# Cached grouped-query attention on one core: where the last V block stands among the wo loads

## The chip, the core and the metric

The kernel runs on one core of a Trainium2 chip. A core has five engines with instruction queues of their own: TensorE (PE, matrix products), VectorE (DVE), ScalarE (ACT), GpSimd (POOL) and SyncE (SP). Here SP issues nearly every load from HBM. The metric is the device time of one execution in microseconds. Before the change its median over 6 runs is 189.66 us (189.29 to 191.03).

## The reference

```python
B, Sq, D = 8, 4, 512;  Hq, Hkv, Sk, Dh = 32, 8, 2048, 128
q = (x @ wq).reshape(B, Sq, Hq, Dh).transpose(0, 2, 1, 3)
k = jnp.repeat(k_cache, 4, axis=1)          # (B, 32, 2048, 128)
v = jnp.repeat(v_cache, 4, axis=1)
p = softmax(einsum("bhqd,bhkd->bhqk", q, k) * Dh ** -0.5)
o = einsum("bhqk,bhkd->bhqd", p, v)
out = o.transpose(0, 2, 1, 3).reshape(B, Sq, Hq * Dh) @ wo      # (8, 4, 512)
```

All inputs are bf16. The two caches are 33.6 MB each and wq and wo are 4.2 MB each, so some 75.5 MB have to be read.

## The kernel before, in words

The work is cut into 32 units of one batch entry and one pair of kv heads; unit u has pair p = u // 8 and batch b = u % 8. Each unit needs one K block and one V block of 1 MB. A software pipeline (the loop at L488) runs step n with three units in hand: PE transposes the K block of unit n (L215; DVE and ACT copy the result out of PSUM, L216), unit n-1 gets its scores and their exponential (L286, L296) and its probabilities are turned to keys (L306), and unit w = n-2 gets the product with V (`values`, L343, for the last twenty units) and is scaled into oT (`finish`, L354). `norms` (L328, L336) makes the reciprocal sums for two units at a time.

The output projection with wo is folded into this loop by quarters of 1024 rows of wo, one for each pair p. `to_tokens` (L428 transposes, L434 copy) and `to_wo_rows` (L450 transposes, L452 copy) bring oT into the row order in which wo is loaded; each needs the one before it. `project(p, r0, n)` (L480) then issues two matmuls for each of n row groups, all of them accumulating into the one PSUM tile out_ps. The last ones are followed by one copy on ACT (L542) and two stores of 16 KB (L543, L544).

Quarter 0 of wo is laid out in three pieces: wo_e (eight small loads early in the kernel), and what is called its last small rows here: wo_n (64 rows, 64 KB, L141) and wo_m (640 rows, 640 KB, L142), both loaded by `load_wo_m`. Quarters 1 to 3 lie in wo_sb. `load_wo(p, r0, n)` (L148) loads n of the eight row groups of quarter p. Quarter 1 and quarter 2 come in two loads of 512 KB each (called 1a, 1b, 2a, 2b here), quarter 3 in four of 256 KB (3a to 3d).

All of these loads stand in SP's one queue in the order in which the program issues them. A list `loads`, built ahead of the loop (L153 to L163), fixes that order for K, V, and some of the wo loads; `load_ready` (L165) issues from it at each step as far as buffers allow (seven K, six V). SP also waits before each load until the load eight places before it has landed: there are eight completion semaphores for loads, used in turn. So about eight loads are always outstanding. The end of SP's order before the change is

```
... V28, K31, V29, V30, V31, wo_n, wo_m, 1a, 1b, 2a, 2b, 3a, 3b, 3c, 3d, output store
```

The order of work on each engine is written by hand: the pool is set to a manual schedule (L71), and an engine runs its instructions in program order. At the end of the loop, step w = 30 issues `values(30)`, `norms(30)`, `finish(30)` and then, on L531 to L533, `project(0, 8, 6)` (rows of wo_m and wo_n, 12 matmuls) and `project(1, 0, 8)` (16 matmuls). Only then comes step w = 31 with `values(31)`, the consumer of V31. After the loop come `to_tokens(2)`, `to_wo_rows(2)`, and the projections of quarters 2 and 3 (32 matmuls).

Of the kernel before, what the change touches and what calls it, by code (L numbers as in the profile page):

```python
# [14 lines left out]
def kernel(  # L15
# [27 lines left out]
    NU = G2 * B  # L43
# [3 lines left out]
    KA = A + 1  # L47
# [85 lines left out]
    def load_wo_e(i):  # L133

        hi, m = divmod(i, 4)
        rows = wo[: NE * WE, :].rearrange("(q r) j -> q r j", r=WE)
        a, b = hi * 32 + m, hi * NE // 2 + m
        nc.sync.dma_start(wo_e[a : a + 17 : 4, :, :], rows[b : b + 17 : 4, :, :])

    def load_wo_m():  # L140
        nc.sync.dma_start(wo_n[:, :], wo[HP * 128 - WN : HP * 128, :])  # L141
        nc.sync.dma_start(  # L142
            wo_m[:, :, :], wo[NE * WE : HP * 128 - WN, :].rearrange("(q r) j -> q r j", r=WM)
        )

    def load_wo(p, r0, n):
        rows = wo[p * HP * 128 : (p + 1) * HP * 128, :].rearrange("(q r) j -> q r j", r=WR)
        nc.sync.dma_start(wo_sb[:, p - 1, r0 : r0 + n, :], rows[:, r0 : r0 + n, :])  # L148
# [4 lines left out]
    loads = []  # L153
    for u in range(NU + KA):
        if 1 <= u <= 8:
            loads.append(("e", u - 1))
        if 0 < u < NU:
            loads.append(("k", u))
        if u == NU + 2:
            loads += [("m", 0), ("w", 0), ("w", 4)]  # L160
        if u >= KA - 1 and u - KA + 1 < NU:
            loads.append(("v", u - KA + 1))
    loads.reverse()  # L163

    def load_ready(nk, nv):  # L165

        while loads:
            kind, u = loads[-1]
            if kind in "emw":
                loads.pop()  # L170
                load_wo_e(u) if kind == "e" else load_wo_m() if kind == "m" else load_wo(1, u, 4)
                continue
            if u >= (nk + KB if kind == "k" else nv + VB):
                return
            loads.pop()
            (load_k if kind == "k" else load_v)(u)
# [30 lines left out]
    def transpose_part(u, part):  # L207
        t, half = divmod(part, 2)
        if half == 0:
            kt[(u, t)] = ktpool.tile([128, JT, 128, 2], BF16, tag="kt", name="kt")  # L210
        kp = psum_k.tile([128, JT // 2, 128], FP32, tag="k", name="kp")
        k4 = ks[u][:, :, :].rearrange("s c d -> s (c d)").bitcast(FP32)
        for j in range(JT // 2):
            w = (part * JT // 2 + j) * 128
            nc.tensor.transpose(kp[:, j, :], k4[:, w : w + 128], ident4[:, :])  # L215
        (nc.scalar.copy if part == 3 else nc.vector.tensor_copy)(  # L216
            out=kt[(u, t)][:, half * JT // 2 : (half + 1) * JT // 2, :, :].rearrange(
                "k j s e -> k (j s e)"
            ),
            in_=kp[:, :, :].rearrange("k j s -> k (j s)").bitcast(BF16),  # L220
        )
# [93 lines left out]
    def sums_by_query(u):  # L315
        by_gq = small.tile([128, 2, 2, HQ], FP32, tag="by_gq", name="by_gq")
        nc.vector.tensor_tensor(
            out=by_gq[:, :, :, :],
            in0=l_sbs[u][:, :].unsqueeze(2).unsqueeze(2).to_broadcast([128, 2, 2, HQ]),
            in1=by_q[:, :, :].unsqueeze(1).to_broadcast([128, 2, 2, HQ]),  # L320
            op=mybir.AluOpType.mult,
        )
        by_qs[u] = by_gq
# [100 lines left out]
    def to_tokens(n):  # L424
        rows = len(groups[n]) * T
        nat = psum_l.tile([rows, HP, 128], BF16, tag="l", name="nat")
        for h in range(HP):
            nc.tensor.transpose(  # L428
                nat[:, h, :], oT[n][:, h, :, :, :].rearrange("d p b s -> d (p b s)"), ident[:, :]
            )  # L430
        flat = nat[:, :, :].rearrange("t h d -> t (h d)")
        nats[n] = nat_sb[:rows, : HP * 128 + (n == 0) * 24 * WE]
        if n > 0:
            nc.vector.tensor_copy(out=nats[n][:, :], in_=flat)  # L434
            return

        w = 32 * WE
        nc.vector.tensor_copy(out=nats[0][:, :w], in_=flat[:, :w])
        nc.vector.tensor_copy(
            out=nats[0][:, w : 2 * w], in_=flat[:, NE // 2 * WE : NE // 2 * WE + w]  # L440
        )
        nc.vector.tensor_copy(out=nats[0][:, 2 * w :], in_=flat[:, NE * WE :])

    def to_wo_rows(n):
        rows = len(groups[n]) * T
        if n > 0:
            perm = psum_l.tile([128, WR, rows], BF16, tag="l", name="perm")
            by_row = nats[n][:, :].rearrange("t (q r) -> t r q", r=WR)
            for r in range(WR):
                nc.tensor.transpose(perm[:, r, :], by_row[:, r, :], ident[:rows, :rows])  # L450
            to = oP3[:, :, :] if n == 2 else oP12[:, :, :, :].rearrange("q r p t -> q r (p t)")
            nc.vector.tensor_copy(out=to, in_=perm[:, :, :])  # L452
            return

        perm = psum_l.tile([128, WE + WM + 1, T], BF16, tag="l", name="perm")
        w = 64 * WE
        by_row = nats[0][:, :w].rearrange("t (q r) -> t r q", r=WE)
        for r in range(WE):
            nc.tensor.transpose(perm[:64, r, :], by_row[:, r, :], ident[:T, :T])
        by_row = nats[0][:, w : w + 128 * WM].rearrange("t (q r) -> t r q", r=WM)  # L460
        for r in range(WM):
            nc.tensor.transpose(perm[:, WE + r, :], by_row[:, r, :], ident[:T, :T])
        nc.tensor.transpose(perm[:WN, WE + WM, :], nats[0][:, w + 128 * WM :], ident[:T, :T])
        nc.vector.tensor_copy(out=oN[:, :], in_=perm[:WN, WE + WM, :])
        nc.vector.tensor_copy(out=oE[:, :, :], in_=perm[:64, :WE, :])
        nc.vector.tensor_copy(out=oM[:, :, :], in_=perm[:, WE : WE + WM, :])

    def project(p, r0, n):

        for r in range(r0, r0 + n):  # L470
            if p > 0:
                o, w = oP[p][:, r], wo_sb[:, p - 1, r]
            elif r < WE:
                o, w = oE[:, r, :], wo_e[:, r]
            elif r < WE + WM:
                o, w = oM[:, r - WE, :], wo_m[:, r - WE]
            else:
                o, w = oN[:, :], wo_n
            for half in range(2):
                nc.tensor.matmul(  # L480
                    out_ps[half * T : (half + 1) * T, :],
                    lhsT=o,
                    rhs=w[:, half * DH : (half + 1) * DH],
                    start=(p == 0 and r == 0),
                    stop=(p == G2 - 1 and r == WR - 1),
                )

    for n in range(NU + A):  # L488
        w = n - A
        for part in range(2):  # L490
            if 0 < n < NU:
                transpose_part(n, part)
        if 2 <= w <= NU - NS and w % 2 == 0:
            finish2(w - 2)
        if 0 < w < NU - NS and w % 2:
            sums_by_row(w - 1)
        if 0 <= n - 1 < NU:
            scores(n - 1)
        for part in range(2, 4):
            if 0 < n < NU:  # L500
                transpose_part(n, part)
        if w >= NU - NS and w % 2 == 0:
            sums_by_query(w)
        if 0 <= n - 1 < NU:
            probs_to_keys(n - 1)
        if w >= 0:
            p, b = units[w]
            if p in (1, 3) and b == 1:
                to_tokens(p // 2)
            if w >= NU - NS:  # L510
                values(w)
                if w % 2 == 0:
                    norms(w)
                finish(w)
            elif w % 2 == 1:
                values2(w - 1)
            if p in (1, 3) and b == 2:
                to_wo_rows(p // 2)
        load_ready(min(n + 1, NU), max(w + 1 if w >= NU - NS else (w + 1) // 2 * 2, 0))
        if w == NU - 1 - VB:  # L520
            assert not loads
            load_wo(2, 0, 4)
            load_wo(2, 4, 4)
            for r in range(0, WR, 2):
                load_wo(3, r, 2)

        if w == 13:
            out_ps = psum_e.tile([2 * T, DH], FP32, tag="e", name="out_ps")
        if 14 <= w < 18:
            project(0, (w - 14) * 2, 2)  # L530
        if w == NU - 2:  # L531
            project(0, WE, WM + 1)
            project(1, 0, 8)  # L533

    to_tokens(2)
    to_wo_rows(2)
    project(2, 0, 4)
    project(2, 4, 4)
    for r in range(0, WR, 2):
# [35 lines left out]
```

## Time and profile before

| what | value |
|---|---|
| median of 6 runs | 189.66 us |
| the profiled execution itself | 196.64 us |
| its span, first to last instruction | 194.9 us |
| PE, DVE, ACT busy | 143.7, 132.4, 62.4 us |
| bytes moved by DMA, mean rate over the span | 75.86 MB, 389 GB/s |
| rate from 0 to 80 us, from 80 to 177 us | 384 GB/s, 425 GB/s |
| rate from 177 to 184.5 us | 377 GB/s |
| granted TensorE clock, mean | 0.959 |

Times in the views are microseconds from the start of the span. "PE kp L215" is an instruction of PE that writes tile kp, recorded for line 215. In a timeline a row has its start, its length, engine, line, operation, output and inputs, the number of instructions that were merged, and in brackets how long the engine had been idle before and what ended that. A load's row on SP is its issue; it lands later. The profiled execution is 7.0 us longer than the median, so differences are worked out in it and then taken from the median.

### The profile page before, as it was taken

The numbers are of one execution on the slowest core, as the hardware profiler recorded it, in microseconds if no ns is written. First come the engines' busy times: TensorE is split into PE (matmuls) and PEld (weight loads), VectorE is DVE, ScalarE is ACT, GpSimd is POOL, SyncE is SP. The second block draws the span as 40 slices with busy tenths as digits, with TensorE's granted clock in tenths as the row PEclk, the third lists the DMA queues.
The fourth block names the chain that finished last, engine by engine and source line by source line (L and its number), as shares of the span: only waits on it lengthen the run. The fifth ranks groups of instructions, "written<-read, shape, count | busy, mean of one in ns | idle before, by whom it ended". The sixth has DMA issues, their size and how long they took to land.

```text
span 194.9 us, 4854 instructions
## 1 busy us (share of the span) xinstructions
PE 143.7 (74%) x2090; PEld 114.7 (59%) x2090; DVE 132.4 (68%) x260; ACT 62.4 (32%) x110; POOL 4.6 (2%) x9
## 2 busy tenths in 40 slices
PE   0706699798885979998787887777777787874673
PEld 0602167677674767887666666666666576763362
DVE  0840459978866579787978785878787887886020
ACT  2011245443523343434333333333333332432000
POOL 8000000000000000000000000000000000000000
PEclk9999999999999699999999999999999999998585
DMA  6999999999999999999999999999999999999940
GB/s 254 432 403 391 392 382 394 382 394 385 392 383 394 382 394 380 415 425 424 422 424 429 425 425 425 425 419 427 422 429 424 429 422 429 424 428 379 380 182 7
DMA packets 10980, 75.86 MB, mean 389 GB/s; under 512 B 1288, under 2 KB 1448, under 8 KB 2600
## 3 DMA queue, kind: packets, MB, share of 16 engines
q1 hardware_dynamic: 10912, 75.55, 95.8%
q8 instruction: 16, 0.26, 0.5%
q14 instruction: 4, 0.03, 0.0%
q10 hardware_dynamic: 48, 0.02, 0.0%
HBM read 75.53 MB, written 0.03 MB: 388 GB/s over the span
## 4 chain that ended last, share of the span: by engine, by line
DMA 92%; PE 4%; SPq 1%; DVE 0%; issue 0%; ACT 0%
DMA k_sb<-in_k_cache_dram 51%; DMA v_sb<-in_v_cache_dram 26%; DMA wo_sb<-in_wo_dram 8%; DMA wq_sb<-in_wq_dram 7%; PE out_ps L480 2%; PE kp L215 1%; SPq L118 1%; PE o_ps L343 0%; DVE nat_sb L434 0%; PE perm L450 0%; PE nat L428 0%; PE s_ps L286 0%; ACT out_sb L542 0%; SPq L128 0%; DVE oT L354 0%
## 5 line engine op out<-in xcount | busy, mean ns | idle before, releaser
L215 PE MATMUL kp<-ident,k_sb 128*128 128x128 f32 x512 | 72.2, 288 | 29.7 <-DMA k_sb<-in_k_cache_dram 28.7
L215 PEld LDWEIGHTS kp<-ident,k_sb 128*128 128x128 f32 x512 | 58.4, 147 | 40.9 <-issue 19.0
L216 DVE COPY kt<-kp 128x1024 bf16<-128x1024 bf16 x96 | 63.2, 687 | 26.1 <-PE kp L215 25.8
L306 DVE STREAM_TRANSPOSE probs<-s_sb 64x512 bf16<-64x512 bf16 x64 | 44.9, 702 | 0.6
L296 ACT ACTIVATE s_sb<-s_ps 128x512 bf16<-128x512 f32 x32 | 19.1, 598 | 72.5 <-PE s_ps L286 72.5
L216 ACT COPY kt<-kp 128x1024 bf16<-128x1024 bf16 x32 | 32.4, 1013 | 16.8 <-PE kp L215 16.8
L286 PE MATMUL s_ps<-kt,q_bd 128*32 128x256 bf16 x512 | 21.1, 282 | 0.0
L343 PE MATMUL o_ps<-probs,v_sb 128*128 128x32 bf16 x640 | 19.2, 176 | 1.5 <-DMA v_sb<-in_v_cache_dram 1.5
L343 PEld LDWEIGHTS <-v_sb 128*128 128x128 bf16 x640 | 18.6, 96 | 2.6 <-DMA v_sb<-in_v_cache_dram 2.0
L286 PEld LDWEIGHTS <-q_bd 128*32 128x32 bf16 x512 | 10.7, 95 | 5.6 <-issue 4.5
L381 PE MATMUL o_ps<-v_sb,probs 128*64 128x256 bf16 x192 | 12.0, 279 | 0.0
L381 PEld LDWEIGHTS <-probs 128*64 128x64 bf16 x192 | 10.3, 112 | 1.2 <-issue 1.0
L354 DVE TENSOR_TENSOR oT<-o_ps,r_sb 128x32 bf16<-128x32 f32 x20 | 3.8, 191 | 7.7 <-PE o_ps L343 7.1
L401 ACT ACTIVATE o_sb<-o_ps,r_sb 128x256 f32<-128x256 f32 x6 | 2.8, 474 | 11.7 <-DVE r_sb L399 11.7
L296 ACT ACTIVATION_READ_ACCUMULATOR s_sb<-s_ps 128x1 f32 x32 | 6.2, 194 | 0.0
L336 DVE RECIPROCAL r_sb<-l_ps 128x64 f32<-128x64 f32 x10 | 5.6, 557 | 0.3
L480 PE MATMUL out_ps<-wo_sb,oP 128*32 128x256 bf16 x48 | 5.2, 390 | 0.2 <-DMA wo_sb<-in_wo_dram 0.2
L252 DVE COPY qT_all<-qtp 128x128 bf16<-128x128 bf16 x8 | 1.2, 217 | 5.8 <-PE qtp L246 5.8
L542 ACT CAST out_sb<-out_ps 64x256 bf16<-64x256 f32 x1 | 0.4, 366 | 14.9 <-PE out_ps L480 14.9
L410 PE MATMUL f_ps<-fold,o_sb 128*128 128x64 f32 x24 | 3.7, 279 | 1.6 <-ACT o_sb L401 1.6
L227 PE MATMUL xtp<-ident,x_sb 32*128 32x32 bf16 x4 | 0.3, 194 | 6.2 <-DMA x_sb<-in_x_dram 6.2
L410 PEld LDWEIGHTS f_ps<-fold,o_sb 128*128 128x128 f32 x24 | 3.1, 190 | 2.4 <-ACT o_sb L401 2.1
(59 smaller groups left out, 65.1 us busy)
## 6 DMA issues: line engine op xcount, KB each, us to landing
k_sb<-in_k_cache_dram SPq DMA_DIRECT2D x32, 1024.0 KB, 19.5
v_sb<-in_v_cache_dram SPq DMA_DIRECT2D x32, 1024.0 KB, 14.2
wq_sb<-in_wq_dram SPq DMA_DIRECT2D x1, 4096.0 KB
wo_sb<-in_wo_dram SPq DMA_DIRECT2D x4, 512.0 KB
wo_sb<-in_wo_dram SPq DMA_DIRECT2D x4, 256.0 KB, 8.6
wo_m<-in_wo_dram SPq DMA_DIRECT2D x1, 640.0 KB
wo_e<-in_wo_dram SPq DMA_DIRECT2D x8, 40.0 KB
wo_n<-in_wo_dram SPq DMA_DIRECT2D x1, 64.0 KB, 18.0
```

The source lines that it names most:

```text
L215: nc.tensor.transpose(kp[:, j, :], k4[:, w : w + 128], ident4[:, :])
L216: (nc.scalar.copy if part == 3 else nc.vector.tensor_copy)(out=kt[(u, t)][:, half * JT // 2 : (half + 1) * JT // 2, :, :].rearrange("k j s ...
L286: nc.tensor.matmul(s_ps[y * 32 : (y + 1) * 32, t * JT : (t + 1) * JT, :], lhsT=q_bd[:, p, e, b, y // 2, :, :], rhs=kt[(u, t)][:, :, y * 32 ...
L296: nc.scalar.activation(out=s_sb[:, :, :], in_=s_ps[:, :, :], func=EXP, accum_out=l_sbs[u][:, u % 2 : u % 2 + 1],)
L306: nc.vector.transpose(out=pr[rows, :, g, :], in_=s_sbs[u][rows, :, :].rearrange("q j s -> q (j s)"))
L336: nc.vector.reciprocal(r_sb[:, :, :], l_ps[:, :, :])
L343: nc.tensor.matmul(o_ps[:, :], lhsT=vs[u][:, c, :], rhs=pr[:, c, :, :].rearrange("s g q -> s (g q)"), start=(c == 0), stop=(c == C - 1),)
L354: nc.vector.tensor_tensor(out=oT[(p + 1) // 2][:, :, (p == 2) * 1, b, :], in0=o_pss[u][:, :].rearrange("d (h s) -> d h s", h=HP), in1=r_sb ...
L381: nc.tensor.matmul(o_ps[i * 64 : (i + 1) * 64, :], lhsT=probs[(u + i) % len(probs)][:, c : c + 2, :, :].rearrange("s c g q -> s (c g q)"), ...
L401: nc.scalar.mul(out=o_sb[:, :, :].rearrange("q c d -> q (c d)"), in_=o_ps[:, :], mul=r_sb[:, 0:1])
L410: nc.tensor.matmul(f_ps[:, :, :].rearrange("d u q -> d (u q)"), lhsT=o_sbs[u][:, c, :], rhs=fold[:, c, :, :].rearrange("k u q -> k (u q)") ...
L480: nc.tensor.matmul(out_ps[half * T : (half + 1) * T, :], lhsT=o, rhs=w[:, half * DH : (half + 1) * DH], start=(p == 0 and r == 0), stop=(p ...
```

## The change

The loads of wo_n and wo_m move one place forward in SP's queue, ahead of V31 instead of behind it. Loads 1a and 1b leave the list `loads` and are issued right behind it, with 2a to 3d; their place is still behind V31. On PE, `project(1, 0, 8)` leaves the step w = 30 and is cut in two: its first four row groups come after the transposes of `to_tokens(2)`, its last four after those of `to_wo_rows(2)`. `project(0, 8, 6)` stays ahead of `values(31)`. No instruction is added or taken away: PE, DVE, ACT and SP issue the same ones as before.

```diff
@@ the list of loads
-        if u == NU + 2:
-            loads += [("m", 0), ("w", 0), ("w", 4)]
+        if u == NU + KA - 2:
+            loads.append(("m", 0))
         if u >= KA - 1 and u - KA + 1 < NU:
             loads.append(("v", u - KA + 1))
@@ load_ready
-            if kind in "emw":
+            if kind in "em":
                 loads.pop()
-                load_wo_e(u) if kind == "e" else load_wo_m() if kind == "m" else load_wo(1, u, 4)
+                load_wo_e(u) if kind == "e" else load_wo_m()
                 continue
@@ the loop
         if w == NU - 1 - VB:
             assert not loads
+            load_wo(1, 0, 4)
+            load_wo(1, 4, 4)
             load_wo(2, 0, 4)
             load_wo(2, 4, 4)
@@ its end, and what follows it
         if w == NU - 2:
             project(0, WE, WM + 1)
-            project(1, 0, 8)
 
     to_tokens(2)
+    project(1, 0, 4)
     to_wo_rows(2)
+    project(1, 4, 4)
     project(2, 0, 4)
     project(2, 4, 4)
```

The end of SP's order after the change is

```
... V28, K31, V29, V30, wo_n, wo_m, V31, 1a, 1b, 2a, 2b, 3a, 3b, 3c, 3d, output store
```

and that of PE's is values(30), project(0, 8, 6), values(31), to_tokens(2), 1a's rows, to_wo_rows(2), 1b's rows, 2a to 3d.

## The prediction

> **What bounds the kernel now.** I read the page's slices first, then the chain that ended last in order of time, then the timeline of the last 18 us.
>
> ```profile
> PEclk9999999999999699999999999999999999998585
> DMA  6999999999999999999999999999999999999940
> GB/s 254 432 403 391 392 382 394 382 394 385 392 383 394 382 394 380 415 425 424 422 424 429 425 425 425 425 419 427 422 429 424 429 422 429 424 428 379 380 182 7
> ```
>
> The sixteen DMA engines are full until the last three slices of 4.9 us. Until then only bytes count, and this change moves none. What can be won lies at the end, where the transfers stop and the core is still at work. The rate also says why this execution took 196.64 us and not 189.66: 384 GB/s until 80 us, 425 after it. 80 x (1 - 384/425) is 7.7 us, more than the whole difference of 7.0, so that lies in the head, and the tail can be taken as it stands.
>
> ```profile
> 169.46 14.93 DMA wo_sb<-in_wo_dram
> 184.40 0.04 issue
> 184.44 1.04 PE out_ps L480 x8
> 185.47 0.94 PE o_ps L343 x32
> 186.41 0.02 issue
> 186.44 0.20 DVE oT L354
> ...
> 188.07 0.67 PE perm L450 x8
> 188.74 3.07 PE out_ps L480 x32
> 191.82 0.02 issue
> 191.84 0.37 ACT out_sb L542
> ```
>
> The chain leaves the DMA with load 1b, which lands at 184.40. From there PE and DVE alone set the end, 7.4 us to the copy at 191.84. `values(31)` stands behind the 1b matmuls on PE, so it starts at 185.41.
>
> ```profile
> 177.02 0.96 PE L343 MATMUL o_ps<-probs,v_sb 128*128 128x32 bf16 x32 [0.85 <-DMA v_sb<-in_v_cache_dram]
> 181.71 1.25 PE L480 MATMUL out_ps<-wo_m,oM 128*32 128x256 bf16 x10 [3.46 <-DMA wo_m<-in_wo_dram]
> 183.21 1.04 PE L480 MATMUL out_ps<-wo_sb,oP 128*32 128x256 bf16 x8
> 185.41 0.99 PE L343 MATMUL o_ps<-probs,v_sb 128*128 128x32 bf16 x32
> ```
>
> PE idles 3.46 us for wo_m. V31 is in the core by then: a load waits for the one eight places before it, so SP's issues tell landings. 3a (176.99) waits for V30, 3b (179.83) for V31, 3d (181.69) for wo_m. V31 therefore lay unused for 185.41 - 179.83 = 5.6 us.
>
> ```profile
> 179.83 0.81 SPq L148 DMA_DIRECT2D wo_sb<-in_wo_dram  x2
> 180.20 0.43 SPq L148 DMA_DIRECT2D wo_sb<-in_wo_dram  x1
> 181.69 0.33 SPq L148 DMA_DIRECT2D wo_sb<-in_wo_dram  x1
> ```
>
> The trace's landing records (the last of sixteen increments of a load's semaphore) fill in the rest: V30 176.98, V31 179.81, wo_n 180.13, wo_m 181.67, 1a 183.02, 1b 184.40, 2a 185.67, 2b 186.90, 3a 187.52, 3b 188.14, 3c 188.76, 3d 189.38. The page has one of them as 8.6 us after issue: 180.20 + 8.6 = 188.8, which is 3c. So the last bytes are there 2.4 us before the copy starts. These 2.4 us, less the last four matmuls, are all that an order of work can win.
>
> **The change, part by part.** *Loads.* wo_n took 0.32 us of the stream (179.81 to 180.13) and wo_m 1.54. Placed behind V30 they land at 177.30 and 178.84, and V31 1.86 us later than now, at 181.67. From 1a on every load has the same bytes ahead of it and keeps its time. SP issues as many loads, and each still waits for the eighth before it; five megabytes and more stay outstanding, so the small wo_n taking a place earlier leaves no hole. V31 also waits for its buffer, free once `values(25)` is done; the present issue at 159.69 shows it free two places sooner than it will be asked for. Cost of this part: V31 late by 1.86 us, hidden while nothing needs it before 181.67, otherwise one for one.
>
> *A rule against it.* The Trainium skill, "DMA: Bandwidth & Descriptors" (Anatomy of one DMA), puts some 2.0 us of fixed time on each DMA, fitted there on the GpSimd path, with bytes over 436 GB/s on top, and its rules for authors call transfers under 64 KB mostly overhead. By that, wo_n (64 KB) costs 2.15 us and wo_m 3.5, and V31 lands at 185.5. By the rows here the two cost 1.86 us, since eight loads overlap their fixed parts. I take the rows; the rule's number is the slow rival's.
>
> *PE, step w = 30.* `project(0, 8, 6)` can start at 178.88 instead of 181.71. Its 12 matmuls took 1.50 us (181.71 to 183.21) at the half clock, so they end by 180.4, and PE waits for V31 with nothing behind it that could run.
>
> *PE and DVE, from V31.* `values(31)` takes 0.99 (185.41 row) whatever the clock: that row lies across the rise of the clock at 185.65, and matmuls came as fast before as after. 181.71 to 182.70. oT 0.19 plus gaps as now: transposes of nat at 182.97. These took 0.62 at full clock; at half I allow 1.0 (bounds 0.62 and 1.24): 183.97. The nat_sb copy, 0.68, runs to 184.69. Under it lie the eight matmuls of 1a, landed at 183.02. At half clock eight took 1.04 from first start to last end, 0.42 of it the last one's own length, so a pair starts every 0.21 and eight hold PE 0.85: 183.75 to 184.6. Their cover is the DVE copy; without it they would cost 0.85. Perm transposes 0.67: 184.74 to 185.4. Their copy to oP3 (0.29) lies under 1b's eight matmuls, to 186.2 (1b landed at 184.40).
>
> *The last 32 matmuls.* At the half clock each eight take 0.85, or start with their load. 2a 186.2 to 187.05 (landed 185.67), 2b to 187.9 (186.90), 3a, four in 0.43, to 188.33, 3b to 188.75, 3c from 188.80 (188.76) to 189.2, 3d from 189.42 (189.38). PE has caught up with the loads with about 0.2 us to spare. The last four end 0.21 + 0.42 later: 190.07. The copy starts at 190.1 instead of 191.84: 1.75 us less.
>
> *The clock.* It was granted at half from 179.0 to 185.65, in full to 189.2 and at half again, in steps of 6.65 and 3.55 us. "TensorE: Matmul & The Clock Gate" (Part 1) says that the clock falls after an idle window of some 3.4 us and returns after a busy one, and that the windows run free. By this PE, mostly busy from 181.7 on, has its full clock from about 185.8 to the end, and the last four end 0.4 after 3d: 189.82, 2.0 us less. But the row shows a fall at 189.2 after a window in which PE was busy 2.54 of 3.60 us, so less than a whole idle window sufficed. I take half clock as the safe case; the two differ by 0.25 us, since the loads hold PE in both.
>
> *Sum.* -1.75 (half clock) to -2.0 (full). A tail that runs at the 425 GB/s of the stretch before it, and not at 377, has 3d land 1.1 us sooner after V30 (12.4 x 0.9 = 11.3), while the old chain, 7.4 us fixed after 1b, comes 0.7 sooner: -2.3 then. I take -1.85: **187.8 us**.
>
> **The rivals.**
>
> *Slower: the small loads hold V31 back.* From the start of `values(31)` the old path to the copy takes 6.43 us (185.41 to 191.84), and 1b's matmuls add 0.85. It decides from a start at 191.84 - 7.28 = 184.55, which is a landing 2.85 us later than 181.67; past that it is lost one for one. With the rule's 185.5 the copy is at 192.8: +0.95, **190.6 us**. For it: V30 to V31 took 2.83 us where V29 to V30 took 2.64, so loads near the small ones do run slower. Against: the small loads' own 1.86 us.
>
> *No change that can be measured: PE falls behind the loads.* If transposes and `values` run slower at the half clock than I allow (nat 1.24, perm 1.0, values 1.5), the matmuls get to 2a 1.1 us later. Nothing catches up, the end comes 0.9 later, and the gain is 0.85: **188.8 us**. For it: half clock for 6.65 us, and only 0.2 us of slack. Against: the unchanged pace of `values` across the rise.
>
> *The order does nothing.* If the last loads set the end already, nothing moves: **189.7 us**. Against: 3d is there 2.4 us early, and the chain does not pass through it.
>
> *More: the tail's loads run at 425 GB/s in ordinary executions*, and PE keeps up: -2.3, **187.35 us**. For it: this execution was the slow kind.
>
> **How the numbers follow.** Forecast 0.76, faster tail 0.08, PE behind 0.09, nothing 0.03, slower 0.04. About 0.5%, 0.95 us, is what a measurement of this kernel can tell from no change. PE behind lies on that border and goes to "same" with the third case: faster 0.84, same 0.12, slower 0.04. The range takes in the fast tail with 0.3 for the spread of medians, and PE behind: 187.05 to 188.8.
>
> **What would show it.** V31 lands after wo_m, near 4.7 us after V30. The idle time of PE ahead of the wo_m matmuls is under 1 us instead of 3.46, and a new one of about 1.3 stands ahead of `values(31)`. That starts 3.7 us earlier against V30's landing. The 1a matmuls lie under the nat_sb copy. The chain leaves the DMA at 3d, with four matmuls and the copy behind it, or still shows PE without a gap from V31 on, if the clock stays at half. I am wrong if V31 lands over 2 us later than wo_m plus its own bytes (2.8), if 3d lands later than 12.4 us after V30, or if PE reaches 3d after it has been there for over half a microsecond.

## The result, and the profile after

The changed kernel takes 188.93 us (median of 28 runs), the kernel before 190.95 in the 63 runs that stand beside it; in some executions of either the loads of the first 80 us run slower, so the comparison is made on the undisturbed ones: a ratio of 0.9939, 95% interval 0.9915 to 0.9962. That is 0.6% less, or 1.2 us. The shortest executions are 188.42 and 189.29. The forecast was 187.8 (0.990 of 189.66) with a range up to 188.8, so the sign was right and the gain was put too high.

The profiled execution of the changed kernel takes 191.62 us, with a span of 189.8. The end of its chain of work, in order of time (start, length, what):

```profile
161.97 16.90 DMA v_sb<-in_v_cache_dram
178.87 0.02 issue
178.89 7.44 DMA wo_sb<-in_wo_dram
186.33 0.04 issue
186.37 0.41 PE out_ps L480 x4
186.78 0.02 issue
186.81 0.37 ACT out_sb L545
```

The chain now stays with the loads until 3d, the last one, at 186.33. Behind it lie four matmuls and the copy, nothing else. In the first trace of before it left the loads at 1b, and seven steps of PE and DVE came between that landing and the copy.

The timeline of PE in the changed kernel:

```profile
174.88 1.03 PE L343 MATMUL o_ps<-probs,v_sb 128*128 128x32 bf16 x32 [1.33 <-DMA v_sb<-in_v_cache_dram]
175.75 0.67 PE L328 MATMUL l_ps<-by_gq,ones 128*128 128x64 f32 x2
176.48 1.25 PE L480 MATMUL out_ps<-wo_m,oM 128*32 128x256 bf16 x10
177.66 0.40 PE L480 MATMUL out_ps<-wo_n,oN 64*32 64x256 bf16 x2
178.92 1.03 PE L343 MATMUL o_ps<-probs,v_sb 128*128 128x32 bf16 x32 [0.86 <-DMA v_sb<-in_v_cache_dram]
...
182.66 3.47 PE L480 MATMUL out_ps<-wo_sb,oP 128*32 128x256 bf16 x36
186.37 0.40 PE L480 MATMUL out_ps<-wo_sb,oP 128*32 128x256 bf16 x4 [0.24 <-DMA wo_sb<-in_wo_dram]
```

The wait of 3.46 us for wo_m is gone. `values(31)` starts at 178.92, 4.1 us after V30 has landed (174.84 by the landing records) and not 8.4 us after it as in the first trace of before. PE reaches 3d with 0.24 us in hand.

The windows of the same tail (length, busy time of PE, PEld, DVE, ACT, POOL, then clock, DMA share, GB/s):

```profile
175.00:178.90 3.90, 3.00 (x46) 2.10 (x44) 1.67 (x4) 0.00 (x0) 0.00 (x0) 0.50 1.00 413
178.90:182.66 3.76, 3.46 (x56) 2.85 (x56) 0.87 (x2) 0.00 (x0) 0.00 (x0) 0.50 0.98 387
182.66:186.33 3.67, 3.48 (x38) 2.40 (x37) 0.29 (x1) 0.00 (x0) 0.00 (x0) 0.65 0.45 175
```

PE had half its clock from 174.97 to 185.21, nearly all of this, and the end still came with the loads.

### The profile page after: what moved, and what is told of

It reads as the page before. It is cut to its first block, busy times and chain, and to the rows that moved or that the text cites. A ratio compares the mean times of both kernels' runs of the same rounds, so it can differ in the third digit from the quotient of the medians.

```text
span 189.8 us, 4854 instructions
## 1 busy us (share of the span) xinstructions
PE 143.3 (76%) x2090; PEld 114.8 (60%) x2090; DVE 132.0 (70%) x260; ACT 62.4 (33%) x110; POOL 4.6 (2%) x9
## 4 chain that ended last, share of the span: by engine, by line
DMA 96%; PE 1%; SPq 0%; issue 0%; ACT 0%
DMA k_sb<-in_k_cache_dram 58%; DMA v_sb<-in_v_cache_dram 27%; DMA wq_sb<-in_wq_dram 7%; DMA wo_sb<-in_wo_dram 4%; PE kp L215 1%; SPq L118 0%; PE s_ps L286 0%; PE out_ps L480 0%; ACT out_sb L545 0%; SPq L128 0%
## 5 line engine op out<-in xcount | busy, mean ns | idle before, releaser
L381 PE MATMUL o_ps<-v_sb,probs 128*64 128x256 bf16 x192 | 11.6, 274 | 0.0
L401 ACT ACTIVATE o_sb<-o_ps,r_sb 128x256 f32<-128x256 f32 x6 | 2.8, 474 | 11.3 <-DVE r_sb L399 11.3
L243 ACT ACTIVATE q_nat<-psq 128x512 bf16<-128x512 f32 x2 | 1.2, 597 | 10.3 <-PE psq L236 10.3
```

The source lines that it names most:

```text
L381: nc.tensor.matmul(o_ps[i * 64 : (i + 1) * 64, :], lhsT=probs[(u + i) % len(probs)][:, c : c + 2, :, :].rearrange("s c g q -> s (c g q)"), ...
L401: nc.scalar.mul(out=o_sb[:, :, :].rearrange("q c d -> q (c d)"), in_=o_ps[:, :], mul=r_sb[:, 0:1])
```

## The experiments

Two theories were set against each other. The clock theory: the tail of the kernel before is a path on PE whose length depends on where the half-clock stretches fall; the first trace showed a long one, most executions have a shorter one, so there was less to win. The load theory: the new order of loads costs something that the sum left out. The tables below use three distances from each trace: V30's landing to 3d's, 1b's landing to the start of the copy to out_sb, and 3d's landing to that copy. Landings are the last of sixteen increments of a load's semaphore.

**The kernel before and the changed one, once more.** No edit.

> The kernel before, once more, for a second trace of its tail. Clock theory: the path after load 1b runs partly at the full clock in most executions, since the clock's windows fall elsewhere; in the first trace the copy to out_sb started 2.46 us after 3d had landed, and this trace should show a shorter distance, 1.2 to 2.2 us, and another clock between 1b and the end. Load theory: the old order of loads is simply good, and the distance stays at 2.3 to 2.6 us. The time itself is 1.000 of the kernel before, within 0.3%, in both.

> The changed kernel, once more. Both theories: 0.994 of the kernel before (0.990 to 0.997). Clock theory: the copy starts 0.4 to 0.7 us after 3d has landed whatever the clock does, and V30 to 3d takes 11.3 to 12.4 us. Load theory: V30 to 3d is longer than in the traces of the kernel before.

Measured: before_again 1.0057 of itself (1.0020 to 1.0095), where 1.000 within 0.3% was expected. A ratio from one such set of executions can thus be off by 0.6%, and smaller differences have to be read from traces. after_again 0.9932 (0.9901 to 0.9962), shortest execution 188.32 where the kernel before had 189.16 beside it. The end of before_again's chain:

```profile
186.22 0.69 DVE nat_sb L434
186.91 0.05 issue
186.96 0.67 PE perm L450 x8
187.63 1.87 PE out_ps L480 x32
189.50 0.02 issue
189.53 0.37 ACT out_sb L542
```

The same 32 matmuls that took 3.07 us in the first trace took 1.87 here, and no other step of the two chains differs by as much as 0.1 us. 1b to copy is 6.30 us instead of 7.44, and the copy starts 1.31 us after 3d instead of 2.46. In after_again the copy starts 0.47 us after 3d, as in the first trace of that kernel. The clock theory said 1.2 to 2.2 and 0.4 to 0.7.

**The order of loads alone.** PE keeps its old order. (Against the kernel before; the lines of `load_ready` are left out.)

```diff
-        if u == NU + 2:
-            loads += [("m", 0), ("w", 0), ("w", 4)]
+        if u == NU + KA - 2:
+            loads.append(("m", 0))
@@
         if w == NU - 1 - VB:
             assert not loads
+            load_wo(1, 0, 4)
+            load_wo(1, 4, 4)
```

> The new order of loads with the old order on PE: all of quarter 1 is projected ahead of values(31). Clock theory: values(31) still waits for 1b, which lands when it did, so nothing is won: 0.997 to 1.003 of the kernel before. Load theory: the new order delays 1b and all that follows it by 0.7 us, and since the path from 1b to the end is unchanged the kernel is slower than before by that, 1.003 to 1.005.

Measured: 1.0029 (0.9977 to 1.0082), shortest execution 189.46. Nothing is won. The ratio doesn't separate the theories, but the landings do. V28 lands ahead of every load that changes its place. From its landing to that of 3d this trace has 19.25 us, and a trace of the kernel before (before_look1, below) has 19.42. The new order of loads does not delay the last landing. The clock was at half all through its tail:

```profile
178.33:183.00 4.67, 3.57 (x56) 2.71 (x55) 0.87 (x2) 0.00 (x0) 0.00 (x0) 0.50 0.62 239
183.00:186.71 3.71, 3.67 (x35) 2.35 (x33) 0.29 (x1) 0.00 (x0) 0.00 (x0) 0.50 0.00 0
```

1b to copy was 8.38 us and the copy 3.36 us after 3d. With that order on PE, whichever the order of loads, the traces without added work have paths from 6.3 to 8.4 us.

**The order on PE alone.** The loads keep their old order.

```diff
             project(0, WE, WM + 1)
-            project(1, 0, 8)
 
     to_tokens(2)
+    project(1, 0, 4)
     to_wo_rows(2)
+    project(1, 4, 4)
```

> The new order on PE with the old order of loads: values(31) follows the wo_m and wo_n matmuls, which still wait for wo_m behind V31. Clock theory: values(31) starts 1.5 us later than in the changed kernel, the matmuls of quarters 2 and 3 are 0.7 to 1.5 us behind the loads at the end, and the gain is a part of that of the whole change: 0.996 to 0.999 of the kernel before. Load theory: without the delay of the loads this is the better half, as fast as the changed kernel or faster: 0.990 to 0.994.

> The new order on PE with the old order of loads, for a second trace. Clock theory: the copy starts 0.47 us after 3d if the clock comes back to full by about the landing of 2a, and up to 2.2 us after it if it stays at half, as in its first trace.

Measured: 0.9933 (0.9895 to 0.9971). Taken alone this ratio is what the load theory wrote down; it lies outside the clock theory's 0.996 to 0.999, though its interval reaches into it. But the executions lie in two groups: 6 of 22 at 188.3 to 188.9 us, as fast as the changed kernel, and 8 at 190.0 to 190.6. In both traces PE is late: the copy starts 2.16 us after 3d in the first (pe_only) and 2.08 in the second (pe_only_look, an execution of 190.23 us), as was expected for a clock that stays at half. The windows of the first:

```profile
179.00:182.00 3.00, 2.54 (x44) 1.68 (x43) 0.16 (x1) 0.00 (x0) 0.00 (x0) 0.50 1.03 416
182.00:185.00 3.00, 2.91 (x30) 2.29 (x32) 1.01 (x3) 0.00 (x0) 0.00 (x0) 0.50 0.83 318
185.00:188.80 3.80, 3.76 (x38) 2.56 (x34) 0.00 (x0) 0.00 (x0) 0.00 (x0) 0.55 0.06 22
```

PE is busy from 179.3 on at half clock and is 1.7 us late at the end (2.16 less the 0.47 that the loads allow), which is about the distance between the two groups. That all eight executions near 190.3 have a late PE is not shown: the trace after_again, of the changed kernel, is an execution of 190.16 us too, with the copy 0.47 us after 3d. From V28's landing to the copy the two traces take 21.50 and 21.39 us; the three later traces of the kernel before take 20.70 to 20.78, and the two of the changed kernel 19.99 and 19.74. In the executions that were traced, then, the order on PE alone is 0.7 us behind the kernel before as it usually is: the clock stayed at half for 10.24 us there, against 6.83 in every trace of the kernel before. The order on PE is the half that can win. The other half gives `values(31)` a start so early that half clock is fast enough.

**Filler on PE in the wait for wo_m**, in the kernel before and with the new order on PE.

```diff
+            fill = psum_k.tile([128, 4, 128], FP32, tag="k", name="fill")
+            for _ in range(12):
+                nc.tensor.matmul(
+                    fill[:, :, :].rearrange("d j s -> d (j s)"),
+                    lhsT=ident[:, :],
+                    rhs=probs[0][:, :16, :, :].rearrange("s c g q -> s (c g q)"),
+                    start=True,
+                    stop=True,
+                )
             project(0, WE, WM + 1)
```

> The kernel before, with twelve matmuls of 512 columns into an unused PSUM tile put on PE where it idles for wo_m. They add work and change nothing else. Clock theory: the tail then runs at the full clock, the path from the landing of 1b to the copy falls from 7.44 us (half clock) to about 5.9, and the kernel gets within 0.5 us of the changed one: 0.993 to 0.997 of the kernel before, with the shortest executions near 188.6 us. If the clock has nothing to do with it, the twelve matmuls cost time or nothing: 1.000 to 1.005.

> The new order on PE with the old order of loads, with the same twelve matmuls in the wait for wo_m. Clock theory: what the new order of loads adds to that of PE is slack for a slow clock alone, so with the clock up this is as fast as the changed kernel in nearly all executions: 0.990 to 0.995 of the kernel before, with fewer executions near 190.3 us than without the twelve matmuls. Otherwise, if moving wo_m ahead of V31 counts by itself, it stays behind the changed kernel by 0.5 us or more.

Measured: before_warm 1.0125 (1.0016 to 1.0235) from only 6 executions, the shortest 190.38. That is a miss for the clock theory as it was written, and the interval reaches into the 1.000 to 1.005 of the other case. Its trace shows the clock full until 182.79 and then at half for one window of 3.4 us, in which the last matmuls lie:

```profile
181.73 0.67 PE perm L450 x8
182.40 3.15 PE out_ps L480 x32
185.55 0.02 issue
185.57 0.37 ACT out_sb L551
```

The filler did raise the clock, and 1b's matmuls became faster (0.61 us instead of 1.04). The 32 did not, and 1b to copy was 7.07. In pe_only_warm the clock stayed full until after the end, and its chain is that of the changed kernel:

```profile
175.89 7.42 DMA wo_sb<-in_wo_dram
183.31 0.04 issue
183.35 0.41 PE out_ps L480 x4
183.76 0.02 issue
183.78 0.37 ACT out_sb L552
```

The copy starts 0.47 us after 3d, not 2.1. The ratio is 0.9939 (0.9891 to 0.9986), 6 of 14 executions are at 188.4 to 188.9, and none is between 189.5 and 191. With the clock up, as in this trace, wo_m behind V31 costs nothing.

**Filler in every wait of the tail of the kernel before.** As before_warm, with a helper that issues such matmuls:

```diff
         if w == NU - 2:
+            fill(12)
             project(0, WE, WM + 1)
             project(1, 0, 8)
 
+    fill(1)
     to_tokens(2)
+    fill(3)
     to_wo_rows(2)
```

> The kernel before with matmuls into an unused PSUM tile in every wait of PE's tail: twelve ahead of the wo_m rows as in before_warm, one ahead of the transposes of to_tokens(2), three under its copy. In before_warm the clock fell again between values(31) and the last matmuls, and 1b to copy took 7.07 us. Clock theory: with these waits filled the clock stays full to the end and 1b to copy takes 5.6 to 6.2 us, 0.2 to 0.7 us more than the loads allow; the shortest executions are at 188.7 to 189.4 us, and the ratio is 0.993 to 0.999. If the clock doesn't matter, 1b to copy stays at 7 us or more.

Measured: 0.9935 (0.9900 to 0.9970), shortest execution 188.80, 12 of 22 at or below 189.3. The windows around 1b's landing (181.07) and the copy (186.86):

```profile
181.07:183.50 2.43, 2.10 (x49) 1.71 (x50) 0.19 (x1) 0.00 (x0) 0.00 (x0) 1.00 0.87 339
183.50:186.86 3.36, 3.30 (x44) 2.26 (x43) 0.97 (x2) 0.00 (x0) 0.00 (x0) 1.00 0.22 84
```

The clock is full to the end, 1b to copy is 5.79 us and the copy starts 0.80 us after 3d. Sixteen matmuls that compute nothing bring the kernel before to within 0.5 us of the changed one by their shortest executions (188.42 and 188.32). The path's dependence on the clock is thus shown by setting it, not only by traces that differ.

**Two more traces of the kernel before.** No edit.

> The kernel before, for a third trace of its tail. Clock theory: from the landing of 1b to the copy it takes between 6.2 us (mostly full clock) and 8.4 (half clock throughout, as the load_only run had it), by how the half-clock stretches fall; the loads themselves take 11.7 to 12.0 us from V30 to 3d. Otherwise it is 7.4 us as in the first trace, whatever the clock.

> The kernel before, for a fourth trace of its tail. As for the third: 6.2 to 8.4 us from 1b to the copy, shorter the longer the clock is full after 1b has landed.

Measured: 1b to copy 6.29 us in both, copy 1.31 us after 3d in both, V30 to 3d 11.88 and 11.95, all within what the clock theory wrote. The first (before_look1) is an execution of 189.54 us, in the middle of the six that the forecast started from; the second (before_look2) is one of 196.93 us, as long as that of the first trace, with the same tail. The end of before_look1's chain:

```profile
159.10 16.91 DMA wo_m<-in_wo_dram
176.00 0.04 issue
176.05 3.48 PE out_ps L480 x27
179.53 0.98 PE o_ps L343 x32
...
182.17 0.68 PE perm L450 x8
182.84 1.87 PE out_ps L480 x32
184.71 0.02 issue
184.74 0.37 ACT out_sb L542
```

In this chain PE is busy without a gap from the landing of wo_m on; so it is in before_again and before_look2. Only in the first trace did PE have to wait for 1b (0.18 us), which landed 7.42 us after V30 there and 6.84 to 6.96 after it in the other three. The windows that hold the last 32 matmuls, of the first trace and then of before_look1, have the clock at 0.59 and at 1.00:

```profile
188.67:191.84 3.17, 3.13 (x34) 2.08 (x32) 0.29 (x1) 0.00 (x1) 0.00 (x0) 0.59 0.01 3
181.40:184.74 3.34, 2.53 (x40) 2.10 (x40) 0.97 (x2) 0.00 (x1) 0.00 (x0) 1.00 0.12 45
```

So three of four traces of that kernel have a path of 6.3 us, and the one used for the forecast is the exception.

**What the loads alone allow.** The changed kernel with one row group projected for each load.

```diff
-    project(1, 0, 4)
+    project(1, 0, 1)
     to_wo_rows(2)
-    project(1, 4, 4)
-    project(2, 0, 4)
-    project(2, 4, 4)
+    project(1, 4, 1)
+    project(2, 0, 1)
+    project(2, 4, 1)
     for r in range(0, WR, 2):
-        project(3, r, 2)
+        project(3, r + r // 6, 1)
```

> The changed kernel with all loads of wo and only 8 of the last 24 row groups projected, one for each load; 16 row groups are left out of the output. It shows where the loads alone put the end. Clock theory: the changed kernel already ends with the loads, so this is as fast as it, within 0.3 us: 0.990 to 0.996 of the kernel before, and the copy starts 0.35 to 0.7 us after 3d has landed. If PE still sets the end of the changed kernel in most executions, this is faster than it by 0.5 us or more, 0.985 to 0.990.

Measured: 0.9919 (0.9884 to 0.9954), shortest execution 188.46 (188.42 and 188.32 for the changed kernel), copy 0.48 us after 3d. Taking away two thirds of the last matmuls brings nothing: the changed kernel ends with its loads, and with these loads another order on PE has nothing more to win.

**Fewer DMA engines for the last two loads**, a try at a faster version.

```diff
-        nc.sync.dma_start(wo_sb[:, p - 1, r0 : r0 + n, :], rows[:, r0 : r0 + n, :])
+        for q0, q1 in ((0, 120), (120, 128)) if p == 3 and r0 >= 4 else ((0, 128),):
+            nc.sync.dma_start(wo_sb[q0:q1, p - 1, r0 : r0 + n, :], rows[q0:q1, r0 : r0 + n, :])
```

> The changed kernel with loads 3c and 3d cut by partitions into 120 and 8, so that each goes to fewer DMA engines. In the trace of the changed kernel the last of the sixteen increments of 3d comes 1.23 us after the one before it, so one DMA engine is late. If that one is among those that the 120 partitions leave out, the end comes 0.5 to 1.0 us earlier than in the changed kernel: 0.986 to 0.991 of the kernel before. If it is another, or if two more loads cost more than they save, this is as fast as the changed kernel or slower by up to 0.5 us: 0.993 to 0.997.

Measured: 0.9984 (0.9933 to 1.0034), shortest execution 189.51, 1.1 us behind the changed kernel's. It is not faster, and ends a little worse than the second case had it. Its trace tells why the first hope failed: the last increment of the 120-partition part of 3d still comes 1.20 us after the one before it (194.69 after 193.49), so the late engine is not the one left out. From V30 to the last landing it takes 12.83 us instead of 11.5, and the loads ahead of the cut ones, 2b to 3b, come later already; why they do is open.

## Why the prediction was wrong in size

| trace | V30 to 3d | 1b to copy | 3d to copy |
|---|---|---|---|
| before, first (used for the forecast) | 12.40 | 7.44 | 2.46 |
| before_again | 11.83 | 6.30 | 1.31 |
| before_look1 | 11.88 | 6.29 | 1.31 |
| before_look2 | 11.95 | 6.29 | 1.31 |
| before_warm | 11.78 | 7.07 | 2.06 |
| before_warm2 | 11.70 | 5.79 | 0.80 |
| pe_only | 11.81 | 7.13 | 2.16 |
| pe_only_look | 11.79 | 7.08 | 2.08 |
| pe_only_warm | 11.76 | 5.46 | 0.47 |
| load_only | 11.56 | 8.38 | 3.36 |
| after | 11.49 | 5.48 | 0.47 |
| after_again | 11.58 | 5.47 | 0.47 |
| after_floor | 11.54 | 5.50 | 0.48 |

The step that failed is the first conclusion drawn from the rates: that the whole difference between the profiled execution and the median lies in the head, "and the tail can be taken as it stands". It could not. Against the trace of an ordinary execution (before_look1, 189.54 us), the span of the first trace is 7.1 us longer, of which 5.4 us lie ahead of V30's landing (176.98 against 171.55) and 1.7 behind it. The 7.7 us of the forecast came from setting 384 GB/s against 425; the first 80 us of before_look1 ran at 413, which makes 5.6. So the head was put too high by about 2 us, and that hid a long tail: 7.44 us from 1b to the copy, where before_look1 has 6.29. The saving was worked out on a long tail and taken from a median of executions that, as far as the traces tell, have the short one. With the short path the sum is 1.31 - 0.47 = 0.84 us, and 189.66 less 0.84 is 188.8. The shortest executions say the same: 189.29 to 188.42 in the first comparison, 189.16 to 188.32 in the second. So do the traces: from V28's landing to the copy it is 20.70 to 20.78 us in the three later traces of before and 19.99 and 19.74 in the two of the changed kernel. The ratio's 1.2 us is larger than 0.84, though its interval (0.7 to 1.6 us) holds it. That some executions of the kernel before do have the long path would add to it, and the first trace shows that they exist; how many do was not measured.

From V30 to the copy the first traces of the two kernels differ by 14.86 - 11.97 = 2.9 us. By the table 1.15 of it is the clock (2.46 to 1.31 after 3d), 0.9 the stretch from V30 to 3d, and 0.84 what the change does in the usual execution. Of the 0.9 only 0.4 is pace, by the time from V28 to 3d (19.93 against 19.51); the rest is that V30 itself lands later after V28 in the new order.

The other steps, by the traces:

- *Loads.* V31 was to land 4.7 us after V30 and came 4.03 after it, behind wo_n (0.25) and wo_m (1.35). The two loads together took 1.60 us where 1.86 was written. The fixed 2 us per DMA of the rule that spoke against the change do not show with eight loads outstanding, and the slow rival falls with it.
- *The last landing.* "From 1a on every load keeps its time" holds: from V28 to 3d it is 19.25 to 19.51 us in the four traces with the new order and uncut loads (after, after_again, after_floor, load_only) and 19.21 to 19.47 in the old one, the first trace apart. V30 to 3d looks some 0.3 us shorter in the new order, but there V30 lands 0.15 us later after V28 (0.5 in the first trace of the changed kernel); why it does is not shown.
- *Rate of the tail.* The rival that the tail's loads run near 425 GB/s came true: behind V30 come 4.92 MB, which take 11.6 us at that rate, and V30 to 3d took 11.5 us against the 12.4 of the first trace. (The forecast's 11.3 for this is a slip: 12.4 x 0.9 is 11.2, and the bytes give 11.6.) But it was given 2.3 us, with the old path at the length of the first trace.
- *PE.* The nat transposes at half clock took 1.03 us (180.24 to the copy's release at 181.27; 1.0 written), 1a's matmuls lie under the nat_sb copy, and the slack at 3d is 0.24 us (0.2 written). The wait ahead of `values(31)` was 0.86 us where 1.3 was written, since V31 came sooner. This part was right.
- *PE falls behind the loads.* It didn't, with half clock until 185.2. It did in both traces of pe_only, where `values(31)` starts 1.5 us nearer to 3d's landing. That is what the moved loads are for.
- *The clock.* The forecast gave the uncertainty of the clock 0.25 us, for the changed kernel, where the loads cover it. It gave it none for the kernel before, where nothing covers it: 6.3 to 7.4 us from 1b to the copy in its four traces. The range was drawn around the same sum and ended at 188.8 for this reason. The clock's times were also read a little off: its records in the first trace put the rise at 185.80 and the fall at 189.21, with stretches of 6.83 and 3.41 us, not 6.65 and 3.55.

## What to carry to other kernels

Before a saving measured in one trace is taken from a median of other executions, ask whether that stretch can differ between executions: here a tail in which PE alone sets the end was over a microsecond longer or shorter by the clock. A change that brings such a path back under the loads also takes that spread away, and its worth is the usual distance to the loads' end, 1.31 - 0.47 us here. When moving work behind a load, look for the load ahead of which it was waiting as well: with wo_m still behind V31, the new order on PE matched the changed kernel in a part of the executions only, and in both traces it ended 1.6 to 1.7 us later than the loads allow.

## What was not expected

- The clock changed in stretches of 3.41 us and multiples of it in every trace. It fell to half after stretches in which PE, by the profile, was busy for more than half the time: in before_warm for 3.41 us from 182.79, after 3.41 us with most of `values(31)` and all the transposes in them, PE busy for 2.35. A wholly idle window isn't needed. Nor does the busy time alone decide. The first trace lost its full clock after a stretch with the same 2.35 us (185.80 to 189.21), and before_look1 kept it after one with 2.35 us too (180.47 to 183.88). The transposes are the same in all three; the two that lost it have 0.60 and 0.68 us of `values(31)` and 0.54 and 0.46 of the projection's matmuls, the one that kept it has 0.02 and 1.11. What the clock counts was not tested.
- `values` takes nearly the same time at both clocks (0.95 to 0.97 us at full, 1.03 to 1.04 at half, for 32 matmuls of 32 columns), while the 32 matmuls of 256 columns take 1.87 us at full clock and 3.55 at half. What the clock costs depends on the shape.
- Useless matmuls in PE's waits made the kernel before faster (0.9935), though the shortest execution, 188.80, stays 0.4 to 0.5 us above those of the changed kernel.
